# Part of the position bias kept in SBUF until the attention, with bias reads, PSUM tiles, clearings and MLP transposes moved

## Chip, core and metric

One core of a Trainium2 chip runs the whole program. The metric is the device time in microseconds of one execution, as the median of several runs; the profile comes from one further execution. Engines are named as in the profile: PE (TensorE), DVE (VectorE), ACT (ScalarE), POOL (GpSimd) and SP (SyncE, which here issues nearly all DMAs).

## The reference, cut to what matters

Three layers follow each other, all in float32: attention with a position bias, an MLP with a layer norm, and a gated MLP.

```python
scores = q @ k.T / sqrt(64)                       # B=4, H=8, S=576, D=64
x = log1p(|i - j|) / log1p(max(i, 1))             # S x S, one row scale per i
bias = relu(x[..., None] @ w1 + b1) @ w2          # hidden 32, one table S x S per head
attn = softmax(scores + bias) @ v                 # to x: 4 x 576 x 512
xn = (x - mu) / sqrt(var + 1e-6) * g_ln
x = x + relu(xn @ w_ch1) @ w_ch2                  # 512 -> 2048 -> 512
h = gelu(x @ w_in); u, v = halves of h            # 512 -> 2 x 512
v_s = w_sg @ layernorm(v) + b_sg                  # mixes the 576 rows
out = x + (u * v_s) @ w_out
```

## The kernel before, in words

The program is one hand-ordered stream for each engine: Python emits the instructions in the order in which each engine runs them, and semaphores order the engines among each other. Products in float32 are made of float32r parts, a high and a low half (`split_hi` on ScalarE, `split_lo` mostly on VectorE), with three matmuls for each product.

**Bias stage** (lines 267 to 447, 0 to 54 us). The table is computed in 36 blocks `z` of 16 rows i, in the order `ORDER`: z = 16 to 23, 8 to 15, 0 to 7, 24 to 35. Step `y` is the place in that order. For each block, four `relu` operations (`units`, L333 on ScalarE, L335 on VectorE) and a few small matmuls (`sums`, L347) make a PSUM tile `pt` of 128 partitions (16 rows x 8 heads), from six banks. `finish(z)` runs a step later: it copies the tile scaled, mirrored to both sides of the diagonal, into an SBUF tile `o` of 128 x 591 (`scaled`, L354 on ScalarE or L356 on VectorE, by the table `EV`) and stores it in a DRAM scratch `scr` (`store`, L368), skewed so that a plain read gives rows of the bias. For z below `FULL` = 24 all eight heads are stored at once, a DMA of 295.5 KB. For z from 24 on `o` is a quarter of a `spare` tile, and only heads 0 and 1 are stored, by `GROUPS` three blocks together at z % 4 == 2 and one at z % 4 == 3, one DMA for each head; a store of all heads of four blocks is put into `M["held"]`. `READ` says after which step `read(k)` (L262, L263, L276, L376) fetches rows 128 k to 128 k + 127 of heads 0 and 1 back into `bias[0]`. SyncE takes all of this in order: a read that has to wait for stores holds back what is behind it. Each DMA also waits for the one that used the same of eight semaphores before.

**Attention** (lines 660 to 955, 54 to 322 us). 16 units, a pair of heads times a batch each, with nine query tiles `n`. The order of the first unit is written out in `FIRST`, that of the others in `SEQ`: `S` scores (L707) into one of two PSUM tiles `s0`, `s1` of two banks each, `add` the bias and take the row's extreme (L713, VectorE), `exp` (L727, ScalarE), `T` transposes (L733) into one of two PSUM tiles, `hi` and `lo` halves, `PV` products into `PB`, `O` transposes into `OB`. A slot `(u, n)` also issues what SyncE has to do there: `place_q` (four copies of the split q into its operand tile), loads of q, k and v for unit u + 2, loads of the next pair's bias at unit 4 p + 2, and at the slots number 2, 3 and 9 (`HELD`) the three held stores. The third frees the spare tiles, whose space then serves the conversion of the MLP's first weights. `bias[1]`, the next pair's bias tile, is allocated when it is first loaded, at unit 2. GpSimd splits q, k and v of the units to come, in order.

The PSUM tiles of the attention are taken over the six banks of the bias stage: `PB`, `OB` and `s0` from bank 4 up, in the order in which they are allocated (L682 to L688), `s1` in banks 2 and 3. A tile may be written once the bias tiles that lay there have been read. Eight clearings of the ends of the `RT` tiles (L673, L674) run on VectorE between the two stages.

**MLP** (lines 1039 to 1185, 322 to about 740 us). The rows lie in five blocks of up to 512. For each block of the first chunk of hidden columns: `h_tile` twice (12 matmuls of 512 columns each, then `relu` and its low half), the first two of the next block's four transposes (`ln_T`, L487, two PSUM tiles in turn, read by `split_hi` and `split_lo`), then four `y_tile` (six matmuls and VectorE's addition L1086), with the third transpose behind the first `y_tile` and the fourth behind the second. The gated MLP fills the rest.

Of the kernel before, what the change touches and what calls it, by code (L numbers as in the profile page):

```python
# [9 lines left out]
F32 = mybir.dt.float32  # L10
# [66 lines left out]
    AA AA AA AA AA AA AA AA AD DD AA DA  # L77
""".split()

READ = {20: [2], 27: [0], 29: [1], 32: [3], 35: [4]}  # L80

FULL = 24
GROUPS = ((3, 2), (1, 3))
HELD = (2, 3, 9)
QK = 5, 16, 11, 22
GATE = 35
STAGES = 8
# [8 lines left out]
def mark(label):  # L96
    pass
# [3 lines left out]
def block_kernel(  # L101
# [6 lines left out]
    act, dve, pool, pe, sp = nc.scalar, nc.vector, nc.gpsimd, nc.tensor, nc.sync  # L108

    def new_pool(name, bufs, stack=None, **kw):  # L110
        return (stack or ctx).enter_context(tc.tile_pool(name=name, bufs=bufs, reuse_waits="tile", **kw))
# [83 lines left out]
    raw, ops, bias, M = {}, {}, {}, {}  # L195
# [4 lines left out]
    M["held_at"] = right.enter_context(ExitStack())  # L200
    M["spare"] = new_pool("aspare", (36 - FULL) // 4, M["held_at"], side="right")
    Qb = [qp.tile([128, 2 * S + 64], F32R, name=f"q{j}") for j in range(2)]
# [49 lines left out]
    def new_bias(hp):  # L252
        bias[hp] = (bp0, bp1)[hp % 2].tile([128, 9, S], F32, name="bias")
# [27 lines left out]
    with ExitStack() as c:  # L281
        p = new_pool("bk", 1, c)
# [31 lines left out]
        )  # L314
        pool.memset(mhalf, -0.5)
        new_bias(0)
        for t in Qb:
            pool.memset(t[:, S:S + 64].bitcast(F32), 0.0)
        def reach(z):

            l, r = 16 * z + 15, S - 16 * z
            return l, r, max(l + 1, r)
# [35 lines left out]
        def store(z, n, src, heads=None):  # L358

            f = 16 + 16 * z * H * PITCH - reach(z)[0]  # L360
            if heads is None:
                dims, src = [[PITCH, 128]], src
            else:
                f += heads * PITCH
                dims, src = [[H * PITCH, 16]], src[heads::H]
            dims += [[16 * (H * PITCH - 1), n], [1, 591]]
            q = act if heads == 1 and z + n > 34 else sp
            q.dma_start(out=bass.AP(scr.tensor, scr.offset + f, dims), in_=src.rearrange("p (s j) -> p s j", s=n))  # L368
# [10 lines left out]

        def finish(z, pts):  # L380
            l, r, n = reach(z)
            if z < FULL:
                t = stg.tile([128, 591], F32, name="o")
            else:
                if z % 4 == 0:
                    spare[z // 4] = M["spare"].tile([128, 4 * 591], F32, name="o")
                t = spare[z // 4][:, 591 * (z % 4):][:, :591]
            left, right = t[:, :l + 1][:, ::-1], t[:, l:]
            for o, pt in pts:
                scaled(EV[ORDER.index(z)][0], z, (right if z < 18 else left)[:, o], pt)  # L390
            if z < 18:
                scaled(EV[ORDER.index(z)][1], z, left[:, 1:], pts[0][1][:, 1:l + 1])
            else:
                scaled(EV[ORDER.index(z)][1], z, right[:, 1:], pts[0][1][:, 1:r])
            if z < FULL:
                store(z, 1, t)
            else:

                for n, at in GROUPS:
                    if z % 4 == at:  # L400
                        for h in range(2):
                            store(z + 1 - n, n, spare[z // 4][:, 591 * (at + 1 - n):591 * (at + 1)], h)
                if z % 4 == 3:
                    M.setdefault("held", []).append(lambda: store(z - 3, 4, spare[z // 4]))
            for k in READ.get(ORDER.index(z), ()):
                read(k)

        spare = {}
# [3 lines left out]
        for y, z in enumerate(ORDER):  # L412
# [19 lines left out]
            if y == QK[2]:  # L432

                KH, KL = (qkp.tile([128, 2, S + 64], F32R, name=n) for n in ("kh", "kl"))
                k = raw[0].pop("k")
# [9 lines left out]
                split_v(0)  # L445
        while late:
            finish(*late.pop(0))


    tiles = [[4 * b + j for j in range(4)] for b in range(B)] + [[16, 17]]  # L450
# [65 lines left out]
    def ln_apply(blk, j):  # L516
        xn[blk][j][1]()
# [28 lines left out]
    side = {}  # L546
# [112 lines left out]
    with ExitStack() as c:  # L659
# [10 lines left out]
        RT = [[atp.tile([128, 2, 320], F32R, name=f"rt{z}{w}") for w in "hl"] for z in range(2)]  # L670

        for t in RT[0] + RT[1]:
            dve.memset(t[:64, :, 288:].bitcast(F32), 0.0)  # L673
            dve.memset(t[64:, :, :32].bitcast(F32), 0.0)  # L674
        AT = [tuple(atp.tile([128, 4, S], F32R, name=f"at{h}{w}") for w in "hl") for h in range(2)]
        pp = new_pool("ap", 1, c)
        Psb = pp.tile([128, 2, S], F32, name="psb")
# [4 lines left out]
        M["rc"] = c.enter_context(ExitStack())  # L682
        psP = new_pool("psP", 1, c, space=PSUM, side="right")
        PB = psP.tile([128, 512], F32, name="PB")
        OB = psP.tile([128, 512], F32, name="OB")
        SB = [psP.tile([128, 2, 512], F32, name="s0")]
        M["s1"] = c.enter_context(ExitStack())
        SB.append(new_pool("psS", 1, M["s1"], space=PSUM).tile([128, 2, 512], F32, name="s1"))  # L688
        PA = list(PT)

        def at(u, n):
            return 9 * u + (n if u else FIRST_ORDER.index(n))

        def emit_S(u, n):
            Q, KH, KL, V = ops[u]
            s = SB[at(u, n) % 2]
            if n == 4:
# [11 lines left out]
        def emit_add(u, n):  # L709
            k = at(u, n)  # L710
            s = SB[k % 2]
            ct, mt = CT[k % 3]
# [25 lines left out]
        def emit_RT(u, n, z):  # L738
            p = SB[(9 * u + n + z) % 2][:, 0, 288:416]
            if n == 4:  # L740
# [4 lines left out]
        def tails(u, n, z):  # L745

            p = SB[(9 * u + n + z) % 2][:, 0, 288:416]
            if n == 4:
# [33 lines left out]
        def pv_bank(u, h, x):  # L782
            return SB[0][:, 0] if (u, h, x) == (NU - 1, 1, 1) else PB

# [16 lines left out]
        def emit_O(u, h, t):  # L801
            pe.transpose(OB[:, 128 * t:128 * t + 128], Psb[:, h, place(t)], ident)

        xt = {}

        def emit_Oev(u, h):
            act.activation(Ob[:, h], OB.rearrange("p (a b) -> p a b", a=4), AF.Copy)
            if not h:
# [28 lines left out]
        def emit_Or(u):  # L837
            pe.transpose(PB[:, 288:416], Pr.rearrange("p h c -> p (h c)"), ident)

# [3 lines left out]
        def emit_xr(u):  # L843
            hp, b = UNITS[u]
            w = xp.tile([128, 2 * D], F32, name="xw")
            xr = M["stage"].tile([128, DM], F32, name="t")[:, :D] if u == NU - 1 else xp.tile([128, D], F32, name="xr")
            dve.tensor_scalar(out=w, in0=PB[:, 288:416], scalar1=RC[u % 2][:, 4:5], scalar2=None, op0=ALU.mult)
            pool.tensor_tensor(out=xr, in0=w[:, :D], in1=w[:, D:], op=ALU.add)
# [30 lines left out]
        def emit_slot(u, n):  # L879

            mark(f"att {u}.{n}")
            k = 9 * u + n
            PT[:] = PA[(k + 1) % 2], PA[k % 2]
            hp, b = UNITS[u]
            if n == 0 and u + 1 < NU:
                place_q(u + 1)
            if n == 1 and "last" in M:
                M.pop("last")()
            if n == 5 and u + 2 < NU:
                load_q(u + 2)  # L890
                load_k(u + 2)
            for f in side.pop(k - 1, []) + ([M["held"].pop(0)] if k in HELD else []):
                f()
            if k == HELD[-1]:
                M["held_at"].close()
                conv_first(new_pool("arc", 2, M["rc"]))
            if u == 12 and n == 0:
                open_first()
            if hp < 3 and b == 2 and n in (1, 4, 7):
                load_bias(hp + 1, n // 3)  # L900
# [20 lines left out]
        for u in range(1, NU):  # L921
# [10 lines left out]
            N=lambda u, j: ln_two(j), R=lambda u, j: M.pop(("scale", j))(), P=lambda u, t: ln_apply(1, t), F=lambda u, j: first_split(j), H=lambda u, f, a, b: h_tile(0, 0, f, a, b),  # L932
# [57 lines left out]
    with ExitStack() as c:  # L990
# [125 lines left out]
        for blk in range(5):  # L1116
            mark(f"mlp 0.{blk}")
            if blk == 1:
                M["h0"].close()
                M["cv"] = new_pool("mcv", 2, c)  # L1120
                js = weight_jobs(1)
                bg.extend(job_tasks(js[:2]))
                n1 = len(bg)
                bg.extend(job_tasks(js[2:]))
                rest = len(bg) - n1
            T = [lambda j=j: ln_T(blk + 1, j) for j in range(len(tiles[blk + 1]))] if blk < 4 else []
            N = [lambda t=t: ln_stats(blk + 2, x_sb[:, t]) for t in tiles[blk + 2]] if blk < 3 else []
            for f in range(2 if blk else 0):
                h_tile(0, blk, f)
                if 0 < blk < 4 and f + 2 < len(T):  # L1130
                    ln_apply(blk + 1, f + 2)
                if f == 0:
                    pump(PUMP[blk])
            for f in T[:2]:
                f()
            pump(PUMP[blk])
            if blk == 4:
                break
            for j in range(4):
                y_tile(0, blk, j)  # L1140
                for f in T[2 + j:3 + j] + N[j:j + 1]:
                    f()
                if 2 <= j < 2 + len(N):
                    ln_apply(blk + 2, j - 2)
                pump(PUMP[blk])
# [209 lines left out]
    t = {b: T_groups(b) for b in range(1, B)}  # L1355
# [83 lines left out]
```

## Time and profile before

| | |
|---|---|
| median of 3 runs | 948.04 us (946.66 to 949.64) |
| the profiled execution | 948.56 us, span 946.8 us |
| PE busy | 925.3 us (98%) |
| DVE, ACT, POOL busy | 721.1, 494.8, 424.7 us |
| granted TensorE clock | 9 tenths or more in all 40 slices |
| DMA | 110.23 MB, mean 116 GB/s |

The page gives busy time of each engine over the span, and then the span in 40 slices: each digit is the busy share of a slice in tenths. The queries behind the rows below give the same by stretches, or every instruction in order of time. A row in order of time has its start from the span's begin, its length, engine, line and operation, the output and inputs, and in brackets the idle time of that engine before it with the event that ended it. `SPq` is a DMA that SyncE issues. A row with `x4` merges four instructions that follow each other; its length then reaches from the first to the last.

### The profile page before, as it was taken

The page shows a single profiled execution, that of the slowest core. Times are in us where ns is not written, and L with a number is a line of the kernel's source. Part 1 is how long each engine was busy: PE and PEld are TensorE (multiplying, and loading weights), DVE is VectorE, ACT ScalarE, POOL GpSimd, SP SyncE. Part 2 cuts the span into 40 slices and gives each one's busy share as a digit, 9 for nine tenths or more (in the row PEclk, how much of TensorE's full clock was granted, in tenths as well). Part 3 has the DMA queues.
Part 4 walks back from the last instruction along what each step waited for, and adds up shares of the span by engine and source line. Part 5 has one row for each costly group of instructions (what it writes and reads, how often), then busy time and mean ns, then how long its engine had stood idle before and what let it go on. Part 6 is the DMA issues. An engine that isn't in the chain of part 4 may idle for free. (4 is left out here: it accounts for less than half of the span.)

```text
span 946.8 us, 16011 instructions
## 1 busy us (share of the span) xinstructions
PE 925.3 (98%) x5681; PEld 807.0 (85%) x5681; DVE 721.1 (76%) x1441; ACT 494.8 (52%) x1108; POOL 424.7 (45%) x547
## 2 busy tenths in 40 slices
PE   7779999999999999999999999999999999999998
PEld 3259999999999888888888888888888998989996
DVE  7988999999889677886779797979755656455452
ACT  7978999999998744222222232223132635253340
POOL 0057788978999543332224333333300524133251
PEclk9999999999999999999999999999999999999999
DMA  6878856756663560202122333332322000001001
GB/s 217 287 229 264 271 139 204 237 170 217 174 197 85 170 201 23 77 23 99 45 77 98 123 97 114 97 123 94 105 67 86 41 1 21 26 0 57 1 34 67
DMA packets 57983, 110.23 MB, mean 116 GB/s; under 512 B 10032, under 2 KB 21040, under 8 KB 57648
## 3 DMA queue, kind: packets, MB, share of 16 engines
q1 hardware_dynamic: 57504, 108.64, 36.1%
q8 instruction: 45, 0.74, 0.3%
q10 hardware_dynamic: 400, 0.58, 0.3%
q14 instruction: 34, 0.28, 0.1%
HBM read 71.37 MB, written 28.38 MB: 105 GB/s over the span
## 5 line engine op out<-in xcount | busy, mean ns | idle before, releaser
L124 PE MATMUL psh<-blk,w1h 128*128 128x512 f32 (+1 forms) x640 | 151.4, 368 | 0.0
L176 POOL TENSOR_TENSOR cvl<-cvl,cvt 128x512 f32<-128x512 f32 x44 | 56.9, 1293 | 206.9 <-DVE cvt L173 178.6
L655 ACT ACTIVATE hh<-psh 128x512 fp32r<-128x512 f32 (+1 forms) x80 | 43.9, 552 | 186.3 <-PE psh L124 186.0
L124 PEld LDWEIGHTS psh<-blk,w1h 128*128 128x128 f32 x640 | 113.4, 188 | 20.7 <-DVE hl L656 0.3
L713 DVE CUSTOM_DVE_ANT_0 ct<-s,bias 128x576 f32<-128x576 f32 x144 | 107.2, 753 | 16.4 <-PE s L707 7.5
L727 ACT ACTIVATE a<-ct,sm 128x576 f32<-128x576 f32 x144 | 112.3, 780 | 3.8 <-DVE sm L713 3.2
L1086 DVE TENSOR_TENSOR x_sb<-psy,x_sb 128x512 f32<-128x512 f32 x144 | 97.3, 684 | 9.1 <-PE psy L124 8.6
L656 DVE SCALAR_TENSOR_TENSOR hl<-psh,hh 128x512 fp32r<-128x512 f32 (+1 forms) x80 | 50.5, 633 | 55.7 <-ACT hh L655 54.6
L124 PE MATMUL psy<-w2h,hh 128*128 128x512 f32 x288 | 90.5, 395 | 0.2 <-DVE x_sb L1086 0.2
L124 PE MATMUL psy<-w2l,hh 128*128 128x512 f32 x288 | 89.0, 390 | 0.0
L124 PE MATMUL psy<-w2h,hl 128*128 128x512 f32 x288 | 88.8, 389 | 0.0
L733 PE MATMUL pt<-ident,a 128*128 128x128 f32 x576 | 84.9, 273 | 0.4 <-DVE at0l L120 0.4
L124 PE MATMUL psh<-blk,w1l 128*128 128x512 f32 (+1 forms) x320 | 79.0, 368 | 0.0
L707 PE MATMUL s<-kh,q 128*128 128x288 f32 x320 | 71.8, 314 | 3.9 <-DVE sm L713 2.3
L733 PEld LDWEIGHTS pt<-ident,a 128*128 128x128 f32 x576 | 68.6, 141 | 1.1 <-DVE at0l L120 0.6
L707 PE MATMUL s<-kl,q 128*128 128x288 f32 x320 | 65.9, 295 | 0.0
L124 PEld LDWEIGHTS psh<-blk,w1l 128*128 128x128 f32 x320 | 56.8, 189 | 9.9
L124 PEld LDWEIGHTS psy<-w2l,hh 128*128 128x128 f32 x288 | 54.1, 188 | 11.6
L124 PEld LDWEIGHTS psy<-w2h,hl 128*128 128x128 f32 x288 | 54.1, 188 | 11.5
L124 PEld LDWEIGHTS psy<-w2h,hh 128*128 128x128 f32 x288 | 52.4, 188 | 10.7 <-DVE x_sb L1086 1.0
L177 POOL TENSOR_TENSOR cvw<-cvl,cvw 128x512 f32<-128x512 f32 x44 | 59.9, 1361 | 3.5
L707 PEld LDWEIGHTS s<-kh,q 128*128 128x128 f32 x320 | 49.1, 189 | 6.0 <-DVE sm L713 3.3
(202 smaller groups left out, 2178.2 us busy)
## 6 DMA issues: line engine op xcount, KB each, us to landing
r<-in_moe_w_ch_dram SPq DMA_DIRECT2D x32, 512.0 KB, 4.9
k<-in_k_dram SPq DMA_DIRECT2D x16, 640.0 KB, 5.2
q<-q SPq DMA_DIRECT2D x64, 144.0 KB, 2.5
scr<-o SPq DMA_DIRECT2D x24, 295.5 KB, 3.1
v<-in_v_dram SPq DMA_DIRECT2D x16, 384.0 KB, 3.5
q<-in_q_dram SPq DMA_DIRECT2D x16, 288.0 KB, 3.7
bias<-scr SPq DMA_DIRECT2D x8, 576.0 KB, 5.6
bias<-scr SPq DMA_DIRECT2D x8, 512.0 KB, 5.7
```

Of the source, the lines that this page charges most:

```text
L124: pe.matmul(ps, lhsT=w, rhs=x, start=start and j == 0, stop=stop and j == len(terms) - 1)
L176: pool.tensor_tensor(out=T["l"], in0=T["l"], in1=T["t"].bitcast(F32), op=ALU.mult)
L177: pool.tensor_tensor(out=T["w"], in0=T["l"], in1=T["w"], op=ALU.add)
L655: act.activation(hh[:, f, :n], ps[:, :n], AF.Relu)
L656: dve.scalar_tensor_tensor(out=hl[:, f, :n], in0=ps[:, :n], scalar=0.0, in1=hh[:, f, :n].bitcast(F32), op0=ALU.max, op1=ALU.subtract)
L707: pe.matmul(s[:, x, :288], lhsT=w, rhs=m[:, 288 * x:288 * x + 288], start=j == 0, stop=j == len(prs) - 1)
L713: dve.tensor_tensor_reduce(out=ct, in0=s[:, :, :288], in1=bias[UNITS[u][0]][:, n].rearrange("p (a b) -> p a b", a=2), scale=-0.125, scalar ...
L727: act.activation(weights(n), ct.rearrange("p a b -> p (a b)"), AF.Exp, scale=-1.0, bias=mt, accum_out=SU[u % 2][:, n:n + 1])
L733: pe.transpose(PA[k % 2][:, j], e[:, 128 * j:128 * j + 128], ident)
L1086: dve.tensor_tensor(out=x_sb[:, t], in0=ps, in1=x_sb[:, t], op=ALU.add)
```

## The change

Blocks z = 0 to 7 (rows 0 to 127) are now treated like z from 24 on: only heads 0 and 1 are stored in the bias stage. Their `o` tiles lie in `bias[1]`, which is therefore allocated at the start. Two stores of all heads (z = 0 to 3 and 4 to 7) join the held ones, sorted behind them, at slots 11 and 13. The reads of rows 256 to 383, 128 to 255 and 384 to 511 move to steps 18, 22 and 33. `OB` is allocated behind `s0`. The clearings of the `RT` tiles go from VectorE to GpSimd, where they stand behind the splits of q and v at the end of the bias stage. In the MLP the third and fourth transposes stand behind the second and third `y_tile`.

```diff
--- before.py
+++ after.py
@@ -77,11 +77,17 @@
     AA AA AA AA AA AA AA AA AD DD AA DA
 """.split()
 
-READ = {20: [2], 27: [0], 29: [1], 32: [3], 35: [4]}
+READ = {18: [2], 22: [1], 27: [0], 33: [3], 35: [4]}
 
 FULL = 24
+
+
+def kept(z):
+    return z < 8 or z >= FULL
+
+
 GROUPS = ((3, 2), (1, 3))
-HELD = (2, 3, 9)
+HELD = (2, 3, 9, 11, 13)
 QK = 5, 16, 11, 22
 GATE = 35
 STAGES = 8
@@ -314,6 +320,7 @@
         )
         pool.memset(mhalf, -0.5)
         new_bias(0)
+        new_bias(1)
         for t in Qb:
             pool.memset(t[:, S:S + 64].bitcast(F32), 0.0)
         def reach(z):
@@ -379,10 +386,13 @@
 
         def finish(z, pts):
             l, r, n = reach(z)
-            if z < FULL:
+            if not kept(z):
                 t = stg.tile([128, 591], F32, name="o")
             else:
-                if z % 4 == 0:
+                if z % 4 == 0 and z < 8:
+
+                    spare[z // 4] = bias[1].rearrange("p a b -> p (a b)")[:, 591 * z:591 * z + 4 * 591]
+                elif z % 4 == 0:
                     spare[z // 4] = M["spare"].tile([128, 4 * 591], F32, name="o")
                 t = spare[z // 4][:, 591 * (z % 4):][:, :591]
             left, right = t[:, :l + 1][:, ::-1], t[:, l:]
@@ -392,7 +402,7 @@
                 scaled(EV[ORDER.index(z)][1], z, left[:, 1:], pts[0][1][:, 1:l + 1])
             else:
                 scaled(EV[ORDER.index(z)][1], z, right[:, 1:], pts[0][1][:, 1:r])
-            if z < FULL:
+            if not kept(z):
                 store(z, 1, t)
             else:
 
@@ -401,7 +411,7 @@
                         for h in range(2):
                             store(z + 1 - n, n, spare[z // 4][:, 591 * (at + 1 - n):591 * (at + 1)], h)
                 if z % 4 == 3:
-                    M.setdefault("held", []).append(lambda: store(z - 3, 4, spare[z // 4]))
+                    M.setdefault("held", []).append((z < 8, z, lambda: store(z - 3, 4, spare[z // 4])))
             for k in READ.get(ORDER.index(z), ()):
                 read(k)
 
@@ -445,6 +455,7 @@
                 split_v(0)
         while late:
             finish(*late.pop(0))
+        M["held"].sort(key=lambda x: x[:2])
 
 
     tiles = [[4 * b + j for j in range(4)] for b in range(B)] + [[16, 17]]
@@ -670,8 +681,8 @@
         RT = [[atp.tile([128, 2, 320], F32R, name=f"rt{z}{w}") for w in "hl"] for z in range(2)]
 
         for t in RT[0] + RT[1]:
-            dve.memset(t[:64, :, 288:].bitcast(F32), 0.0)
-            dve.memset(t[64:, :, :32].bitcast(F32), 0.0)
+            pool.memset(t[:64, :, 288:].bitcast(F32), 0.0)
+            pool.memset(t[64:, :, :32].bitcast(F32), 0.0)
         AT = [tuple(atp.tile([128, 4, S], F32R, name=f"at{h}{w}") for w in "hl") for h in range(2)]
         pp = new_pool("ap", 1, c)
         Psb = pp.tile([128, 2, S], F32, name="psb")
@@ -682,8 +693,9 @@
         M["rc"] = c.enter_context(ExitStack())
         psP = new_pool("psP", 1, c, space=PSUM, side="right")
         PB = psP.tile([128, 512], F32, name="PB")
+
+        SB = [psP.tile([128, 2, 512], F32, name="s0")]
         OB = psP.tile([128, 512], F32, name="OB")
-        SB = [psP.tile([128, 2, 512], F32, name="s0")]
         M["s1"] = c.enter_context(ExitStack())
         SB.append(new_pool("psS", 1, M["s1"], space=PSUM).tile([128, 2, 512], F32, name="s1"))
         PA = list(PT)
@@ -889,9 +901,9 @@
             if n == 5 and u + 2 < NU:
                 load_q(u + 2)
                 load_k(u + 2)
-            for f in side.pop(k - 1, []) + ([M["held"].pop(0)] if k in HELD else []):
+            for f in side.pop(k - 1, []) + ([M["held"].pop(0)[2]] if k in HELD else []):
                 f()
-            if k == HELD[-1]:
+            if k == HELD[2]:
                 M["held_at"].close()
                 conv_first(new_pool("arc", 2, M["rc"]))
             if u == 12 and n == 0:
@@ -1138,7 +1150,7 @@
                 break
             for j in range(4):
                 y_tile(0, blk, j)
-                for f in T[2 + j:3 + j] + N[j:j + 1]:
+                for f in (T[1 + j:2 + j] if j else []) + N[j:j + 1]:
                     f()
                 if 2 <= j < 2 + len(N):
                     ln_apply(blk + 2, j - 2)
```

## Rows read from the trace of the kernel before

**Rows 1.** Page, busy tenths of 40 slices of 23.7 us, TensorE

```profile
PE   7779999999999999999999999999999999999998
```

**Rows 2.** Stretches: length, busy us (instructions) by engine, clock, DMA share

```profile
54.00:60.00 6.00, 5.29 (x37) 4.66 (x37) 4.59 (x17) 3.77 (x11) 5.75 (x6) 1.00 0.54 150
60.00:70.00 10.00, 6.79 (x47) 5.59 (x46) 8.08 (x22) 7.48 (x20) 5.84 (x5) 1.00 0.82 263
```

**Rows 3.** In order of time: start, us, engine, line, operation, idle before

```profile
51.80 2.13 DVE L356 TENSOR_SCALAR o<-pt,small 128x63 f32<-128x63 f32 x6
...
52.13 1.18 PE L347 MATMUL pt<-m,W 128*32 128x288 f32 x16 [0.24 <-DVE o L356]
...
53.85 0.27 ACT L354 ACTIVATE o<-pt,small 128x15 f32<-128x15 f32 x1 [1.22 <-DVE o L356]
...
54.17 0.53 PE L707 MATMUL s<-kh,q 128*128 128x288 f32 x2 [0.86 <-ACT o L354]
...
54.54 0.42 PE L707 MATMUL s<-kl,q 128*128 128x288 f32 x2
...
55.01 0.11 DVE L674 MEMSET rt1l<- 64x64 f32 x1
...
55.21 0.76 DVE L713 CUSTOM_DVE_ANT_0 ct<-s,bias 128x576 f32<-128x576 f32 x1
```

**Rows 4.** Groups of one form on GpSimd, 0 to 20 us: busy, mean

```profile
L318 POOL MEMSET q<- 128x64 f32 x2 | 0.2, 146 | 0.0
```

**Rows 5.** GpSimd in order of time, 74 to 91 us

```profile
74.39 0.67 POOL L114 TENSOR_SCALAR q<-q 128x576 fp32r<-128x576 f32 x1 [8.39 <-DMA q<-in_q_dram]
...
88.54 0.67 POOL L114 TENSOR_SCALAR q<-q 128x576 fp32r<-128x576 f32 x1
89.29 1.45 POOL L120 TENSOR_TENSOR q<-q 128x576 fp32r<-128x576 f32 x1
```

**Rows 6.** In order of time, 59 to 65 us, two additions of VectorE

```profile
59.86 0.76 DVE L713 CUSTOM_DVE_ANT_0 ct<-s,bias 128x576 f32<-128x576 f32 x1 [0.55 <-DMA bias<-scr]
...
64.32 0.76 DVE L713 CUSTOM_DVE_ANT_0 ct<-s,bias 128x576 f32<-128x576 f32 x1 [0.46 <-DVE at1l L120]
```

**Rows 7.** SyncE's issues in order of time, 47 to 81 us

```profile
47.71 0.38 SPq L262 DMA_DIRECT2D bias<-scr  x1
...
49.24 2.81 SPq L368 DMA_DIRECT2D scr<-o  x4
55.74 0.36 SPq L376 DMA_DIRECT2D bias<-scr  x1
...
60.28 1.12 SPq L276 DMA_DIRECT2D bias<-scr  x2
...
63.99 1.20 SPq L368 DMA_DIRECT2D scr<-o  x2
66.33 0.35 SPq L210 DMA_DIRECT2D q<-in_q_dram  x1
...
80.50 0.50 SPq L210 DMA_DIRECT2D q<-in_q_dram  x1
```

**Rows 8.** DMA issues, 0 to 110 us: count, KB each, median us to landing

```profile
scr<-o SPq DMA_DIRECT2D x24, 295.5 KB, 3.1
...
q<-q SPq DMA_DIRECT2D x20, 144.0 KB, 2.8
...
scr<-o SPq DMA_DIRECT2D x5, 36.9 KB, 3.6
```

**Rows 9.** TensorE in order of time, first scores of unit 3

```profile
100.63 0.51 PE L707 MATMUL s<-kh,q 128*128 128x288 f32 x2
```

**Rows 10.** TensorE in order of time, MLP, block 1 and start of block 2

```profile
343.62 0.66 PE L487 MATMUL pt<-ident,t 128*128 128x128 f32 x4 [0.34 <-DVE blk L120]
...
350.53 1.98 PE L124 MATMUL psh<-blk,w1h 128*128 128x512 f32 x8
```

**Rows 11.** VectorE in order of time, MLP, third output addition of block 1

```profile
349.29 0.68 DVE L1086 TENSOR_TENSOR x_sb<-psy,x_sb 128x512 f32<-128x512 f32 x1
```

## The prediction

> **What bounds the kernel now.** I read the page's slices first, then the stretches in a table by stage, then the two places where TensorE idles, in order of time, then SyncE's issues. The reader is to see this. TensorE stands at 7 tenths in three slices of 23.7 us and at 9 from the fourth (71 us) on [rows 1]; by stage it lacks 0.71 us of 6.00 between 54 and 60 us and 3.21 us of 10.00 between 60 and 70 [rows 2]. So whatever brings the first attention steps forward ends the kernel earlier by as much, and work moved between other engines is worth nothing by itself. Ahead of 54 us VectorE sets the pace: its last six evictions of the bias table run back to back until 51.80 + 2.13 = 53.93 us [rows 3]; the change takes no arithmetic from them. I therefore cost four edits: the first score tile's start, the reads of bias rows, the held stores, and the MLP's transposes.
>
> **Part 1: PSUM space and clearings, 1.05 us.** The last bias matmul ends at 52.13 + 1.18 = 53.31 us. The first score matmul starts at 54.17, 0.86 us of idle later, and what released it is ScalarE's 15-column copy at 53.85, the very last reader of a bias bank [rows 3]: `s0` is laid over that bank. With `OB` and `s0` exchanged, `s0` lies one bank lower, over the results of the block before the last (z = 33), and the bank read last falls to `OB`, which is first written a unit later. z = 33's evictions stand in VectorE's run ahead of the last two; ending some 2 x 0.4 us before 53.93, they are done at about 53.1, so TensorE goes on at 53.31. The four matmuls of the first tile last from 54.17 to 54.54 + 0.42 = 54.96, 0.79 us; they now end at 54.10. VectorE's first addition starts at 55.21, right behind eight clearings, the last of which ends at 55.12 [rows 3]. Those go to GpSimd, VectorE is free at 53.93, and the addition starts when its tile is there, at about 54.15: 1.05 us earlier. On GpSimd eight clearings at 0.146 (the nearest row, a clearing of the same 64 columns [rows 4]) are 1.2 us ahead of the split of the next unit's k; that engine next waits 8.39 us for a q [rows 5], which covers them. Without that cover they would delay the next unit's k by 1.2 us. Bounds: 0.2 (only the clearings' end counts, 55.21 to about 55.0, if `s0` still lies over the last bank) to 1.05. I take 1.05, since the row names the wait.
>
> **Part 2: keeping six heads, and where the reads stand, 0.9 us.** Eight stores of 295.5 KB (rows 0 to 127, all heads) become four of 110.8 and four of 36.9 KB, heads 0 and 1 alone: 2.36 MB become 0.59 in the bias stage. The store count there stays eight. The read of rows 128 to 255 moves from step 29 to 22 and that of rows 256 to 383 from 20 to 18, so behind rows 0 to 127 no read is left until the one of rows 384 to 511. What that is worth is at two additions. One waits 0.55 us for its bias at 59.86; the one at 64.32 starts 0.46 late, put down to VectorE's own operation before it; that one had ended, so I lay it to the last bias rows, read at 60.28 [rows 6, 7]. SyncE shows why. The read of rows 0 to 127 goes out at 47.71; the four stores of z = 28 to 31, spread over 49.24 to 52.05, come behind it; the read of rows 384 to 511 must wait for those to land and goes out only at 55.74, 4.1 us before 59.86; the last read goes out at 60.28, behind two more stores [rows 7]. With the queue lighter I expect the first at about 46, the stores by 50.5, the third read at 53.5 instead of 55.74, landed at 57.6, while its addition is due at 59.86 - 0.55 - 1.05 = 58.26: no wait. The last read follows at some 57.5 instead of 60.28, well ahead of 64.32 - 0.46 - 1.6 = 62.3. Both waits go, 0.55 + 0.46, less 0.1 for ScalarE, which is nearly full there: 0.9. What is late next is ScalarE and VectorE themselves in the first unit's chain, which I leave as it is. That the third read's step goes from 32 to 33 changes nothing, no store stands between them. Bounds: 0 (the reads go out as before) to 1.0; below nothing only if that read fell behind the store of z = 34, and the code has it ahead.
>
> The Trainium skill's page "DMA: Bandwidth & Descriptors", section Bandwidth, says that transfers under 64 KB are dominated by their descriptors and that one should batch to a MiB; it speaks against cutting stores up. The landing times here agree so far that smaller stores do not land faster: 3.1 us at the median for 295.5 KB, 3.6 for 36.9 KB [rows 8]. By the page this part would be worth nothing and the sum 1.7; by the bytes taken off it is worth 0.9. That is the second rival below.
>
> **Part 3: two held stores more, 0 us.** They move 1182 KB each, at units 1.2 and 1.4, and SyncE reaches them just ahead of unit 3's q read, now issued at 80.50 [rows 7]. The two held stores at 63.99 show their price: the q read behind them, issued at 66.33, is what GpSimd waits for until 74.39 [rows 5, 7], so 10.4 us for 2.36 MB of stores and 0.29 of q, some 3.9 us a store. Two more delay unit 3's q by up to 7.8. GpSimd takes it up at 88.54 without a wait, so it would come at up to 96.3; with 0.67 + 1.45 for its split [rows 5] and 2.8 for the copy into place [rows 8] that is 101.2, against its first use at 100.63 less what parts 1 and 2 give, 98.7 [rows 9]: a stall of 2.5 us at worst. From the other side: the last bias read is some 2.8 us earlier, and all behind it on SyncE with it (q copies, held stores, q reads), and the read at 80.50 may land well before 88.54. I take 0, the nearer end, because both go the same way and the delay spends slack first. The source is unit pair 1's bias tile, unused until its own load in unit 2; that load waits for these stores, and its rows are used at unit 4.
>
> **Part 4: MLP transposes, 0.68 us.** In blocks 1 and 2 the third transpose stands behind the first output tile and waits 0.34 us for VectorE's low half of the first, twice (343.62 and 356.93) [rows 10]. One output tile later (some 1.4 us) that half is long there: 2 x 0.34 = 0.68. What may be late next is the fourth transpose's low half: VectorE had it before its third output addition, which ends at 349.29 + 0.68 = 349.97; now it stands behind it, so it ends there at the latest, the same operations being done. The next block needs it at its ninth matmul, 350.53 - 0.34 = 350.19 [rows 10, 11]: 0.2 us to spare. Gone, it would cost its own lateness, at most 0.6 us, a low half, twice. Bounds -0.5 to 0.68.
>
> **Sum.** 1.05 + 0.9 + 0 + 0.68 = 2.63 us. The profiled execution took 948.56 us (span 946.8 and 1.8 around it), so 945.9; it stands 0.5 above the runs' median of 948.04, so the median becomes 945.4 us.
>
> **The rivals.**
> (a) More goes than two waits: all 3.92 us of TensorE's idle time between 54 and 70 us shrink, the later ones being echoes of the first [rows 2]. With two thirds of the remaining 2 us gone the sum is 4.0, so 944.0. For it: q copies and bias come nearly 3 us earlier. Against: the idle times further on stand at the first unit's own chain.
> (b) The reads go out as before, by count and not by bytes. Then 1.05 + 0.68 = 1.73, so 946.3. If `s0` also keeps a late bank, 0.2 + 0.68 and 947.2. For it: the store count stays. Against: three quarters of the bytes in front of the read at 47.71 are gone, and the next read's way is free of two others.
> (c) Slower: the held stores decide. If unit 3's q lands after about 94 us, TensorE stands at unit 3's first scores; the same backlog meets the bias loads of the next pair and unit 4's q. Two stalls of 2.5, less 2.63: 2.4 us slower, 950.4; it decides from some 5 us of lateness at 88.54 on. For it: 8.39 us of waiting behind such stores. Against: GpSimd did not wait at 88.54, and the queue runs earlier. The Trainium skill's page "DMA: Bandwidth & Descriptors" ("Issuing engines are not separate DMA queues") says that all transfers share 16 engines; the trace agrees, with the q read's 8.06 us.
> (d) The change doesn't act: the layout puts other bias results under `s0`, and both waits stay; 0.68 alone, 947.4.
>
> **How the numbers follow.** Forecast 0.45, (a) 0.18, (b) 0.17, (c) 0.12, (d) 0.08. Beyond 0.3% (2.84 us, about what a measurement of this kernel tells from no change) lies under 945.2 or over 950.9. The forecast is 0.2 us short of it: with half a us of spread on either side 0.18 of its 0.45 fall under it. Faster: 0.18 + 0.18 and 0.01 = 0.37. Slower: half of (c), where the stalls are longer, and a tail for the unknown, 0.10. The rest, 0.53, within. The range 943.6 to 948.8 takes in (b) and (d) and the bounds of parts 1, 2 and 4; it leaves out most of (c) and the far end of (a).
>
> **What would show it.** Right: the first score matmul at about 53.3 and the first addition at 54.15 us; no addition waiting for bias; the read of rows 384 to 511 out before 54; TensorE full by 68; no wait at the MLP's third transposes. Wrong: TensorE idle before the first scores of units 3 or 4, GpSimd waiting many us for q there, or the 128x15 copy still releasing the first score tile.

## The result and the profile after

The changed kernel takes 953.01 us (median of 5 runs, 952.41 to 954.73), the kernel before 948.04 beside it (945.99 to 949.64). The ratio is 1.0056, 95% interval [1.0043, 1.0068]: slower, where 945.4 was forecast, and outside the range of 943.6 to 948.8.

The profiled execution after, page, head and TensorE's slices:

```profile
span 950.4 us, 16005 instructions
...
PE   6789999999999999999999999999999999999998
```

It is 3.6 us longer than the one before (946.8), and the difference lies in the first slices: 6 and 8 stand where 7 and 7 stood [rows 1]. By stretches (columns as in [rows 2]), first a stretch of the kernel before:

```profile
30.00:54.00 24.00, 19.46 (x191) 5.15 (x183) 23.98 (x66) 21.44 (x51) 1.94 (x3) 1.00 0.88 290
```

and the changed kernel:

```profile
30.00:54.00 24.00, 18.25 (x115) 4.21 (x115) 18.07 (x49) 14.74 (x35) 0.00 (x0) 0.86 0.52 153
54.00:60.00 6.00, 5.57 (x74) 2.87 (x71) 5.29 (x14) 5.08 (x13) 2.58 (x4) 1.00 0.54 152
60.00:70.00 10.00, 8.34 (x57) 6.91 (x56) 8.93 (x21) 8.38 (x20) 9.40 (x15) 1.00 0.68 183
```

Between 60 and 70 us TensorE is busier than before (8.34 against 6.79 us [rows 2]); that is what the forecast looked for, though the attention also starts later here, so the stretches do not hold quite the same work. The loss is ahead of it: between 30 and 54 us VectorE and ScalarE, which build the bias table, are busy 18.07 and 14.74 of 24 us, where they were busy 23.98 and 21.44. The waits of the first 75 us name the place (engine, line, waited for: us in total, times, longest):

```profile
ACT bias L361 <- DMA scr<-bias: 9.3, 2, 6.4
DVE bias L363 <- ACT bias L361: 4.1, 1, 4.1
```

ScalarE's evictions into the kept tile `bias[1]` wait for a store that reads it, and VectorE waits for ScalarE. The trace of before has no wait of an eviction for a DMA. In order of time (start, us, engine, line, idle before):

```profile
37.80 1.06 ACT L361 ACTIVATE bias<-pt,small 128x264 f32<-128x264 f32 x3 [6.43 <-DMA scr<-bias]
...
42.27 0.33 DVE L363 TENSOR_SCALAR bias<-pt,small 128x111 f32<-128x111 f32 x1 [4.10 <-ACT bias L361]
...
45.61 0.90 ACT L361 ACTIVATE bias<-pt,small 128x464 f32<-128x464 f32 x2 [2.83 <-DMA scr<-bias]
...
53.21 0.52 SPq L268 DMA_DIRECT2D bias<-scr  x1
...
57.86 1.18 PE L354 MATMUL pt<-m,W 128*32 128x288 f32 x16 [0.41 <-DVE o L363]
...
58.97 0.54 PE L719 MATMUL s<-kh,q 128*128 128x288 f32 x2
...
60.01 0.76 DVE L725 CUSTOM_DVE_ANT_0 ct<-s,bias 128x576 f32<-128x576 f32 x1 [0.36 <-ACT o L361]
60.02 0.37 SPq L383 DMA_DIRECT2D bias<-scr  x1
...
104.59 0.51 PE L719 MATMUL s<-kh,q 128*128 128x288 f32 x2
```

The 264-column eviction at 37.80 is z = 3, the 464-column one at 45.61 z = 7. The last bias matmul ends at 57.86 + 1.18 = 59.04 us; before it ended at 53.31 [rows 3]: 5.73 later. From that point on the change gains. The first score starts at 58.97, with no idle time (before: 0.86 us), the first addition 0.97 us behind the last bias matmul instead of 1.90, and no addition waits for bias any more [rows 3, 6]. Unit 3's first scores come 104.59 - 59.04 = 45.55 us behind it, before 100.63 - 53.31 = 47.32 [rows 9]: 1.77 us gained. The MLP's third transpose starts without a wait, where it waited 0.34 us twice [rows 10]:

```profile
348.69 0.60 PE L498 MATMUL pt<-ident,t 128*128 128x128 f32 x4
```

So 5.73 - 1.77 - 0.68 = 3.28 us of the 3.6 in the spans are accounted for. The medians lie 4.97 us apart; this execution of the kernel before had a slower start than this one of the changed kernel (granted clock 0.94 against 1.00 in the first 30 us), which run 1 below bears on. The question is what those two waits are, and whether they are all.

### The profile page after: what moved, and what is told of

Read it like the earlier page. It is cut to its first block, busy times and chain, and to the rows that moved or that the text cites. A ratio compares the mean times of both kernels' runs of the same rounds, so it can differ in the third digit from the quotient of the medians.

```text
span 950.4 us, 16005 instructions
## 1 busy us (share of the span) xinstructions
PE 927.3 (98%) x5681; PEld 807.2 (85%) x5681; DVE 719.6 (76%) x1433; ACT 494.0 (52%) x1108; POOL 425.1 (45%) x555
## 5 line engine op out<-in xcount | busy, mean ns | idle before, releaser
L667 DVE SCALAR_TENSOR_TENSOR hl<-psh,hh 128x512 fp32r<-128x512 f32 (+1 forms) x80 | 50.5, 632 | 56.5 <-ACT hh L666 56.5
L126 DVE TENSOR_TENSOR at0l<-pt,at0h 128x512 fp32r<-128x512 f32 (+1 forms) x80 | 49.5, 620 | 6.3 <-ACT at0h L123 5.6
```

The source lines that it names most:

```text
L126: (eng or dve).tensor_tensor(out=o, in0=i, in1=hi.bitcast(F32), op=ALU.subtract)
L667: dve.scalar_tensor_tensor(out=hl[:, f, :n], in0=ps[:, :n], scalar=0.0, in1=hh[:, f, :n].bitcast(F32), op0=ALU.max, op1=ALU.subtract)
```

## The experiments

**What the compiled program says.** z = 3 writes columns from 1773 on of `bias[1]`; the two stores that it waits for read columns 0 to 1772 (z = 0 to 2). z = 7 writes from 4137 on; its stores read 2364 to 4136. Nothing overlaps, and yet the program's list of waits has both evictions wait until these stores have landed. The same pattern of blocks and stores in the tile of z = 24 to 35, which is declared as one row of 4 x 591 columns, has no such wait. `bias[1]` is declared as 9 x 576 columns, and three blocks of 591 without a gap make one run of 1773. If the run is counted in whole rows of 576, 0 to 1772 reaches to 2303 and 2364 to 4136 to 4607, which takes in z = 3 and z = 7. With one unused column between blocks (592), or a store for each block, the waits are not in the program. The rule of whole rows is a guess that fits these two waits; it cannot hold for every store, since the store of z = 3 alone (columns 1773 to 2363) would by it reach to 2879 and take in z = 4, which has no such wait. Why the program waits is open; that it does is read off the program and the trace. The store for each block was not run.

**Theory A**: these two needless waits are the loss, the rest works about as forecast. **Rival B**: the late stage comes from the stores and reads on SyncE, the wait is only where it shows. **Rival C**: TensorE's lower clock in the stage is a cause of its own. Each run's ratio is to the kernel before, timed beside it.

**1. One column between blocks** (a store's access pattern follows the spacing):

```diff
-                    spare[z // 4] = bias[1].rearrange("p a b -> p (a b)")[:, 591 * z:591 * z + 4 * 591]
+                    spare[z // 4] = bias[1].rearrange("p a b -> p (a b)")[:, 592 * z:592 * z + 4 * 592]
```

> The changed kernel with the kept rows of a head spaced 592 columns apart in bias[1] in place of 591: same copies, same stores, same reads; one unused column lies between two blocks. With 591 the program's evictions of z = 3 and z = 7 carry a wait for the two stores of the blocks before them, with 592 they carry none. Theory A (these waits, 6.43 and 2.83 us on ScalarE in the trace of after, lengthen the bias stage by 59.04 - 53.31 = 5.73 us, and the rest of the change works about as predicted): the last bias matmul ends at 53.3 to 53.6 us, no eviction waits for a store, time 945.6 (before less 1.78 and 0.68 us, which the first additions and the MLP gained beside the 5.73) to 947.3 (after less 5.73). Theory B (the late stage comes from the stores' and reads' place on SyncE and from transfers, and the wait is only where it shows): the wait moves to another step, the last bias matmul ends past 57 us, time 951 to 953. Theory C (TensorE's clock, 0.50 to 0.84 of full between 36 and 54 us in after, is a cause of its own): the clock stays below 1.00 there and the stage ends past 55 us, time 948.5 or more.

Measured: 952.23 us (951.22 to 952.89), ratio 1.0037 [1.0024, 1.0051]. Theory A was right about the waits and wrong about the time (945.6 to 947.3). No eviction waits, the clock is 1.00 through the stage, and its last matmul ends at 51.28 + 1.18 = 52.46, 6.58 us earlier than after; but the span, 949.5 us, is only 0.9 shorter. In order of time (SPq and ACTq are the queues that SyncE and ScalarE issue to):

```profile
45.68 0.47 SPq L269 DMA_DIRECT2D bias<-scr  x1
51.28 1.18 PE L354 MATMUL pt<-m,W 128*32 128x288 f32 x16 [0.24 <-DVE o L363]
52.29 0.65 ACTq L375 DMA_DIRECT2D scr<-o  x1
53.29 0.52 ACTq L375 DMA_DIRECT2D scr<-o  x1
54.66 2.48 SPq L375 DMA_DIRECT2D scr<-o  x4
58.66 0.36 SPq L383 DMA_DIRECT2D bias<-scr  x1
62.73 0.76 DVE L726 CUSTOM_DVE_ANT_0 ct<-s,bias 128x576 f32<-128x576 f32 x1 [5.20 <-DMA bias<-scr]
...
63.55 1.33 PE L720 MATMUL s<-kh,q 128*128 128x288 f32 x4 [5.25 <-DVE sm L726]
...
104.34 0.51 PE L720 MATMUL s<-kh,q 128*128 128x288 f32 x2
```

Its waits of SyncE's queue:

```profile
SPq L375 <- DMA scr<-o: 8.4, 1, 8.4
```

SyncE issues nothing from 46.15 to 54.66. Its next store, of z = 28 to 30, waits for a DMA of `o` to land; the one that was on its way is ScalarE's store of z = 32 to 34, issued at 52.29. Rows 384 to 511 can only be read behind the stores (58.66), and the addition at 62.73 waits 5.20 us for them. Unit 3's first scores (104.34) come only 0.25 us earlier than after (104.59): the 6.58 us are lost again. The program shows why a store waits for a later one: a DMA signals its landing on one of eight semaphores given out in turn, and each waits until the last holder of its semaphore has landed. The turn goes by the order in which the program is laid out, and without the needless waits the first of ScalarE's two late stores stands ahead of SyncE's store of z = 24 to 26 in it. Eight places behind it is SyncE's store of z = 28 to 30. In the program of after it stands eight places ahead of the last read, which needs its data anyway. This is **theory D**: behind the first wait stood a second, which the first one's delay had kept out of the program.

The Trainium skill's page "DMA: Bandwidth & Descriptors", section "Why a DMA increments its semaphore by 16 and not by 1", gives a reason for the turn: with two DMAs in flight on one semaphore, a wait for the first can pass on the second's counts, so a semaphore belongs to one transfer at a time. The waits in this program agree; no run here let two share one.

**2. The change without keeping:** `return z >= FULL` in `kept`, three held stores.

> The changed kernel with nothing kept of rows 0 to 127 (all eight heads stored in the bias stage, three held stores): PSUM order, clearings on GpSimd, the reads' new places and the MLP's transposes stay. Theory A (keeping alone carries the loss): the last bias matmul ends at about 53.3 us; 1.05 - 0.12 = 0.93 us from PSUM and 0.68 from the MLP stay, so 946.4; the reads' places bring 0 to 0.9 more, 945.5 to 946.4. Theory B (the reads' new places, ahead of the stores on SyncE, make the loss): 950 to 953, the stage's end past 56 us.

Measured: 947.04 us (945.26 to 949.36), ratio 0.9990 [0.9979, 1.0000]; last bias matmul at 52.80, first score at 52.72. Rival B is refuted: the reads' new places do not make the loss. The time is 0.6 us above what theory A gave for this run (945.5 to 946.4), and one addition waits for bias longer than any did before:

```profile
59.09 0.76 DVE L725 CUSTOM_DVE_ANT_0 ct<-s,bias 128x576 f32<-128x576 f32 x1 [1.21 <-DMA bias<-scr]
```

**3 and 4. The keeping alone, in the kernel before,** with 591 and with 592 columns.

> The kernel before with the keeping alone, as the change writes it (591 columns apart, five held stores); reads, PSUM, clearings and MLP as before. Theory A: the same two evictions wait for stores, the stage's last matmul ends 4 to 6 us later than in before (a read no longer lies ahead of the stores on SyncE, so the waits may be shorter than 6.4 and 2.8), time 952 to 954. Theory B (the reads' places make the loss): at most 1 us from before, 947 to 949.

> As the one before it, with 592 columns in place of 591. Theory A: no wait for a store, the bias stage as in before, its last matmul ends at 53.3 us; the kept heads spare 1.77 MB of stores in the stage, and the waits of additions for bias (0.55 and 0.46 us) go in part: 947.2 to 948.0. The difference to the run with 591 is 4 to 6 us and is one column of spacing. Theory B (the bytes of the held stores, moved to units 3 and 4, cost time there) : 949 to 950.5, with TensorE idle at a first score of unit 3 or 4.

Measured: 956.29 us (954.31 to 959.52), ratio 1.0087 [1.0068, 1.0106], with 591; 952.18 (951.85 to 953.30), 1.0041 [1.0028, 1.0054], with 592. With 591 the waits of the evictions are the same (9.0 us in two), but the loss is larger than expected: the last bias matmul ends at 60.93 us, 7.6 later than before, and the time lies 2.3 us above the 952 to 954. That execution had a granted clock of 0.89 in its first 30 us; what the rest is was not tried. 592 takes the waits away; but here too an addition then waits 4.29 us for bias, and SyncE stands 7.9 us in one wait for a store. The 952.18 was a miss for theory A (947.2 to 948.0) and is what D says. The column is worth 4.1 us here and 0.8 in run 1, less than the stage gains by it in either, since the second wait takes the first one's place.

**5. Both waits away:** 592 columns, and SyncE issues all stores, so that no semaphore is shared between queues.

```diff
-            q = act if heads == 1 and z + n > 34 else sp
+            q = sp
```

> The changed kernel with 592 columns between kept blocks, and with the two stores that ScalarE's queue issues (second head of the last four blocks) issued by SyncE. Theory A alone fell: with 592 no eviction waits, the stage ends in time, and yet the time is 952.2. Theory D: a second wait stood behind the first. With 592 columns the program gives ScalarE's two late stores a completion semaphore that SyncE's store of z = 28 to 30 has after it, so SyncE stands 8.4 us (46.15 to 54.66) until a store has landed that is issued at 52.29, and an addition waits 5.2 us for rows 384 to 511. With all stores on one queue no semaphore is shared across queues. D expects: stores of z = 28 to 31 issued before 51 us, rows 384 to 511 read by 54 us, no addition waiting over 1 us for bias, 945 to 946.5 (the run without keeping, 947.0, less its 1.2 us wait of an addition for bias). Theory E (keeping costs by itself, by the held stores' bytes in units 3 and 4): 949 to 952, with TensorE idle in those units.

Measured: 945.61 us (945.05 to 946.94), ratio 0.9962 [0.9947, 0.9976]. Theory D holds; E (keeping costs by itself) is refuted. In order of time:

```profile
45.00 0.52 SPq L268 DMA_DIRECT2D bias<-scr  x1
...
46.84 3.04 SPq L375 DMA_DIRECT2D scr<-o  x4
51.17 1.18 PE L354 MATMUL pt<-m,W 128*32 128x288 f32 x16 [0.24 <-DVE o L363]
51.31 0.36 SPq L383 DMA_DIRECT2D bias<-scr  x1
52.28 0.53 PE L720 MATMUL s<-kh,q 128*128 128x288 f32 x2
...
53.31 0.76 DVE L726 CUSTOM_DVE_ANT_0 ct<-s,bias 128x576 f32<-128x576 f32 x1 [0.35 <-PE s L720]
...
56.49 1.12 SPq L282 DMA_DIRECT2D bias<-scr  x2
57.35 0.75 DVE L726 CUSTOM_DVE_ANT_0 ct<-s,bias 128x576 f32<-128x576 f32 x1
...
97.84 0.51 PE L720 MATMUL s<-kh,q 128*128 128x288 f32 x2
```

The stores of z = 28 to 31 are out by 49.88, rows 384 to 511 are read at 51.31, the last rows at 56.49, and no addition waits for bias. Unit 3's first scores come 97.84 - 52.35 = 45.49 us behind the last bias matmul, in run 1 104.34 - 52.46 = 51.88: the second wait cost 6.39 us. Once more, in another set of runs:

> The kernel with 592 columns and all stores on SyncE once more, beside new runs of the kernel before. The runs with one part undone came out 2.0 to 2.8 us above its first 945.6, while their traces show 0.88 us (PSUM and clearings), 0.68 (MLP) and about 1.2 (reads) at their own places, and the end of the bias stage itself differs between executions by about 1 us (52.35 against 53.38 us) with the clock of the first 30 us (1.00 against 0.89). If 945.6 was the kernel's own time: 0.996 of before again, 0.9947 to 0.9976. If it was a favourable set of executions: 0.997 to 0.998, 946.5 to 947.5 beside a before of 949.

Measured: 946.25 us (944.45 to 947.90) beside 949.25, ratio 0.9969 [0.9959, 0.9978]. The ratio lies in the first range (0.9947 to 0.9976), but just under the second (0.997 to 0.998), so part of the first gain may have been a favourable set. The kernel beats both others, by 0.3% the one before and by 0.7% or more the changed one.

**6. Each of the two edits without the other.** With 591 columns and SyncE's stores:

> The changed kernel (591 columns) with ScalarE's two stores issued by SyncE. Theories A and D together: the evictions of z = 3 and z = 7 still wait for stores, the stage's last matmul ends at 58 to 59 us as in after; after's rows 384 to 511 are not held by a shared semaphore there, so nothing is gained: 952 to 953.5. If the stores' queue alone were the cause (either wait enough by itself), 947 or less.

Measured: 954.44 us (952.69 to 958.11), 0.9 above the range, ratio 1.0055 [1.0034, 1.0076]. Its stage, its waits, and its last bias matmul:

```profile
30.00:54.00 24.00, 16.47 (x132) 4.33 (x136) 19.42 (x53) 15.01 (x36) 0.00 (x0) 1.00 0.51 153
```

```profile
ACT bias L361 <- DMA scr<-bias: 9.0, 2, 6.2
```

```profile
57.56 1.18 PE L354 MATMUL pt<-m,W 128*32 128x288 f32 x16 [0.67 <-DVE o L363]
```

This run also settles rival C: the granted clock was 1.00 in the whole stage, where after had 0.86, and its last bias matmul ends at 58.74 all the same (59.04 in after). The ratios together:

| | ScalarE issues two stores | SyncE issues all |
|---|---|---|
| six heads kept, 591 columns | 1.0056 (after) | 1.0055 |
| six heads kept, 592 columns | 1.0037 | 0.9962, 0.9969 |
| nothing kept, the rest of the change | 0.9990 | 0.9990 |
| the kernel before | 1 | 0.9998 |

Neither edit brings the gain alone; moving the stores without the keeping does nothing.

**7. SyncE's stores without keeping,** in the kernel before and in the changed one:

> The kernel before with ScalarE's two stores issued by SyncE, nothing else. In the program of before the read of rows 384 to 511 carries a wait for ScalarE's first store too (it has the same semaphore before it): issued at 53.15, landed at about 55.7, and the read follows at 55.74. D expects that read at 53 to 54.5 us, the addition's wait of 0.55 us gone; two more issues of 0.6 us stand ahead of the last rows' read: 947.0 to 948.1. If that read waits for its own rows' stores alone, it stays at 55.7 and the time grows by up to 1.2: 948 to 949.3.

> The changed kernel with nothing kept of rows 0 to 127, and with ScalarE's two stores issued by SyncE. Set against the first of these four it is what keeping six heads is worth when neither wait is there. D expects the 1.21 us wait of an addition gone or below 0.5: 945.8 to 947. Keeping itself (1.77 MB fewer in the stage) is then worth 0 to 1 us; if keeping costs, this one is the faster of the two by 2 or more.

Measured: 949.02 us (947.03 to 951.64), ratio 0.9998 [0.9985, 1.0011], and 948.18 (947.24 to 951.66), 0.9990 [0.9977, 1.0004]. Theory D's times missed in both (947.0 to 948.1 and 945.8 to 947); in the kernel before, the other time named, for a read that waits for its own rows' stores alone (948 to 949.3), is the one that came. In the kernel before, with SyncE's stores (this profiled execution took 951.64 us, the longest of them):

```profile
49.94 2.50 SPq L368 DMA_DIRECT2D scr<-o  x4
56.56 0.36 SPq L376 DMA_DIRECT2D bias<-scr  x1
...
60.84 0.76 DVE L713 CUSTOM_DVE_ANT_0 ct<-s,bias 128x576 f32<-128x576 f32 x1 [1.01 <-DMA bias<-scr]
```

In the changed kernel without keeping, where the wait of an addition was to go below 0.5 us (this profiled execution too was the longest, 951.66 us):

```profile
51.23 2.47 SPq L375 DMA_DIRECT2D scr<-o  x4
57.09 0.36 SPq L383 DMA_DIRECT2D bias<-scr  x1
...
61.49 0.76 DVE L725 CUSTOM_DVE_ANT_0 ct<-s,bias 128x576 f32<-128x576 f32 x1 [2.25 <-DMA bias<-scr]
```

The reads at 56.56 and 57.09 come 4.1 and 3.4 us behind the last of their own rows' stores (52.44 and 53.70); in run 5 that was 1.4 us (49.88 to 51.31). With all eight heads stored, the landing of these stores holds the read about as late as the semaphore does. So the keeping is what makes room: 0.9962 and 0.9969 against 0.9990, 2.0 to 2.7 us, once nothing else holds SyncE.

**8. One part undone in the kernel of run 5.** Part 1 (`OB` ahead of `s0`, clearings on VectorE), part 4 (`T[2 + j:3 + j]`), and the reads' places (`READ` as before):

> The kernel with 592 columns and all stores on SyncE, with part 1 undone: OB and s0 in the old order, the eight clearings on VectorE. Where part 1 works as forecast, undoing it brings back the 0.86 us between the last bias matmul and the first score and puts the first addition 1.90 us behind the last bias matmul in place of 0.96: 945.6 + 0.93 = 946.5. If a later wait hides it: 945.6.

> The same kernel with part 4 undone: the MLP's transposes of the block after next in their old places. The two waits of 0.34 us of TensorE in blocks 1 and 2 come back: 945.6 + 0.68 = 946.3. If they are hidden by what follows: 945.6.

> The same kernel with the reads in their old places (steps 20, 27, 29, 32, 35). If the bytes spared by keeping six heads are what brings the last rows early, the reads' places add little: rows 384 to 511 read at 51 to 53 us, no addition waits over 0.5 us for bias, 945.4 to 946.2. If the places carry part 2, an addition waits 0.5 us or more again: 946.4 to 947.

Measured: 948.45, 947.58 and 947.97 us, ratios 0.9983 [0.9973, 0.9994], 0.9990 [0.9980, 1.0001] and 0.9990 [0.9980, 1.0000], beside 0.9962 and 0.9969 with everything in place. All three are 1.0 to 2.0 us slower than their expectations allowed, and 2.2, 1.3 and 1.7 us above the 946.25 of the second set. Each part seems to count, but intervals as wide as these don't size a part of 0.7 us; the traces do, each counted from its own last bias matmul. Part 1 undone:

```profile
52.34 1.18 PE L354 MATMUL pt<-m,W 128*32 128x288 f32 x16 [0.24 <-DVE o L363]
54.06 0.53 PE L719 MATMUL s<-kh,q 128*128 128x288 f32 x2 [0.54 <-ACT o L361]
...
55.36 0.76 DVE L725 CUSTOM_DVE_ANT_0 ct<-s,bias 128x576 f32<-128x576 f32 x1
...
128.53 0.66 PE L745 MATMUL pt<-ident,a 128*128 128x128 f32 x4 [0.64 <-DVE at0l L126]
```

The first addition comes 1.84 us behind the stage (53.52), in run 5 it was 53.31 - 52.35 = 0.96: 0.88 us. Two waits of 0.6 us, the one shown and one at 145.77, stand neither in before nor in run 5; why was not tried. Part 4 undone, a line of TensorE's waits from 300 us on:

```profile
PE pt L499 <- DVE blk L126: 0.7, 2, 0.4
```

The two waits are back, 0.7 us in all. Reads in their old places, the stores and the read of rows 384 to 511, and two additions:

```profile
47.14 3.04 SPq L375 DMA_DIRECT2D scr<-o  x4
54.08 0.36 SPq L383 DMA_DIRECT2D bias<-scr  x1
...
58.16 0.76 DVE L726 CUSTOM_DVE_ANT_0 ct<-s,bias 128x576 f32<-128x576 f32 x1 [0.44 <-DMA bias<-scr]
...
63.00 0.76 DVE L726 CUSTOM_DVE_ANT_0 ct<-s,bias 128x576 f32<-128x576 f32 x1 [0.85 <-DMA bias<-scr]
```

The read comes 3.9 us behind its stores (50.18 to 54.08), and the additions wait 0.44 and 0.85 us for bias again: fewer bytes alone do not clear the two waits, nor do the places alone (runs 2 and 7). Part 2 needs both.

## Why the prediction was wrong

**The step that failed** stands in the paragraph on what bounds the kernel: "Ahead of 54 us VectorE sets the pace ...; the change takes no arithmetic from them. I therefore cost four edits". Arithmetic was the wrong thing to count. Until then each block of rows 0 to 127 had a tile of its own; the change puts eight blocks into one tile, lets stores read it while later blocks are written to it, and so adds waits to the evictions that set the pace. That term was missing: 9.3 us of waits, of which 6.6 us reach the end of the bias stage (59.04 against 52.46 us in run 1). Run 1 changes the spacing by one column, the waits are gone, and the stage ends 6.58 us earlier. No rival had that term either; the slower one, (c), named the held stores.

**Part 1** (1.05 us) was right in mechanism, and nearly in size: 0.93 in after against before, 0.88 by undoing it.

**Part 2** (0.9 us) was right about what the fewer bytes and the places do, and wrong in expecting "the third read at 53.5": after issues it at 60.02, behind a stage that ends late. In the kernel with neither wait the four times it gave are met or beaten: rows 0 to 127 read at 45.0 (46 forecast), the stores out by 49.9 (50.5), the third read at 51.3 (53.5), the last at 56.5 (57.5). It had looked at SyncE's order and its bytes only. Which transfer's landing a DMA waits for beside its data's, it never asked, and this decided run 1.

**Parts 1 and 2 together**, 1.95 forecast: unit 3's first scores come 1.83 us nearer to the last bias matmul in run 5 (97.84 - 52.35 = 45.49, before 47.32), 1.77 in after.

**Part 3** (0): right. After has no idle time of TensorE at the first scores of unit 3, and in run 5 TensorE is full where the two held stores go out:

```profile
70.00:115.00 45.00, 44.99 (x365) 44.90 (x364) 39.97 (x106) 42.29 (x115) 32.21 (x37) 1.00 0.89 288
```

GpSimd does wait for q there, 12.9 us in three waits, and TensorE does not wait for GpSimd there. The forecast had named such waits of GpSimd as a sign of being wrong; they came and cost nothing. Rival (c) is out. Its price was also too low: if 10.4 us are shared over 2.36 and 0.29 MB, 3.9 us is the price of a megabyte; a store of 1.18 MB is then 4.6, the worst stall 4.0 us in place of 2.5, and (c) 953.4 us. That this is near the measured 953.01 is chance.

**Part 4** (0.68): right, 0.68 by the two waits gone, 0.7 by undoing it.

**The sum.** 1.83 + 0 + 0.68 = 2.5 us of 2.63: by the traces the four edits do what the forecast said once the two waits are away. The times of run 5, 945.61 and 946.25 us, lie near the 945.4 forecast for the change, partly by chance: the kernel before took 949.70 and 949.25 beside them, so they are 4.1 and 3.0 us faster, and the traces account for 2.5 of that. As written, the change pays 5.73 us for a layout that the forecast priced at nothing, and 6.6 against an execution with the same start (run 1, granted clock 1.00 in the first 30 us as in after). With 6.6 the sum is 6.6 - 1.77 - 0.68 = 4.1 us of the 4.97 between the medians; the rest stays open. Rivals (b) and (d) are not what happened: the reads go out early and the first score does not wait in run 5. Nor is (a): it wanted some 3.3 us by the first units, and unit 3 shows 1.83.

## What to carry to other kernels

When a change puts several buffers into one, list for each new writer which readers of its neighbours it now waits for, whatever the columns say; a layout that is one column off can cost more than the transfers it saves. A wait that is removed can change the order in which the program is laid out, and with it which transfers share a completion semaphore: a late DMA on another engine's queue can then hold an early one on this queue, so look for a queue that issues nothing for many us and ask whose landing ended it. Size small parts from the same event in both traces, here the last bias matmul, not from the medians alone.

## What the runs showed of the hardware

TensorE's clock did not follow one rule that could be read off these traces. In run 1, after it had stood from 58.30 to 63.55 us for want of bias, the next stretch had a granted clock of 0.54, near the lower of the two levels (1.2 and 2.4 GHz), and the four matmuls at 63.55 took 1.33 us, where those at the same step took 0.79 before:

```profile
64.00:70.00 6.00, 5.58 (x24) 4.98 (x23) 4.19 (x11) 3.59 (x9) 2.52 (x2) 0.54 0.81 229
```

By unit 3 the loss against run 5 was 6.39 us, so a wait of 5.2 us cost more than itself; that the clock is the rest was not tested apart. Yet the stages of after and of run 6, with the same waits, had 0.86 and 1.00, and ended within 0.3 us of each other: there TensorE was not what set the pace.

Executions of the same code differ by about 1 us by the end of the bias stage: its last matmul ended at 52.35 us in run 5 and at 53.50 in its second profile, with granted clocks of 1.00 and 0.94 in the first 30 us:

```profile
52.32 1.18 PE L354 MATMUL pt<-m,W 128*32 128x288 f32 x16 [0.24 <-DVE o L363]
```

That is the size of the parts weighed here.
